# Two more logits products on GpSimd in place of VectorE, and a new stored order for about 110 other operations

## The chip, the core and the metric

The kernel runs on one core of one Trainium2 chip. The time is that of the core on the device in microseconds (us). A core has five engines that run side by side, each through its own list of instructions in order: TensorE (PE in the profile, with its weight loads as PEld), VectorE (DVE), ScalarE (ACT), GpSimd (POOL) and SyncE (SP). SP, ACT and POOL also issue DMAs, and such a DMA has a place in that engine's list.

## What is computed

For 2048 rows x of 640 numbers, the output is a gated mix of an attention and of a filter in the frequency domain:

```python
g = sigmoid((x * gate_w).sum(-1, keepdims=True))
# a: 32 heads of 20; each row attends to itself and to 7 earlier rows, 2 apart
q, k, v = split(x @ wqkv)
logits[s, w] = q[s] . k[s - 2 * w] * 20 ** -0.5     # w = 0..7, -1e9 where s - 2 * w < 0
a = (softmax(logits) @ v) @ wo
# b: a filter on the 2-D spectrum
b = irfft2(rfft2(x) * (w_r + 1j * w_i), s=(2048, 640))
out = g * a + (1 - g) * b
```

## The kernel before, in words

**Tiles.** Row 16 p + j of x lies on partition p in group j, so there are 16 row groups j of 128 partitions, even ones (par 0) and odd ones (par 1) apart, because attention goes 2 rows back at a time. The 640 columns of q, k and v come in four parts of 160.

**Stages.** First the input is folded and loaded, and from there to about 230 us PE multiplies x by wqkv (tiles qkv, in pairs of a high and a low part for accuracy); ACT copies the results out (ev) and sends them to DRAM (qkvd). `attend(par, h)` then reads k, q and v of half a part back and does the attention of it on DVE, POOL and ACT. Its names carry a number u = 4 * par + h // 2 and a letter, a for even h and b for odd: kt5a, q5a, L5a, pr5a and pv5a belong to (par, h) = (1, 2), those with 5b to (1, 3). From about 230 to 347 us `freq(g)` (line 637) filters frequency group g for g = 1, 2, 3, 0, 4 to 15. Then PE multiplies the filtered rows back (`spatial`) and the attention's output by wo (`project_even`, `project_odd`), and the mix is stored to 453.8 us.

**Logits.** In `attend` the eight rows of a partition go in four steps jj = 0, 2, 4, 6. Each is one product pr of 128x1280 numbers (k by q, line 532 and on), then a reduction on DVE into L. A step listed in the table POOL_PR has its product on POOL, which reads q from SBUF. The others are on DVE: ACT first copies the piece of q into one of three parts of a PSUM bank (qbank), and DVE multiplies from there:

```python
            if jj in POOL_PR.get((par, h), ()):
                mul, qj = G.tensor_mul, q[:, jj : jj + 2]
            else:
                self.qturn = (self.qturn + 1) % 3
                mul, qj = V.tensor_mul, self.qthird[self.qturn]
                A.copy(qj, q[:, jj : jj + 2].rearrange("p j c -> p (j c)"))
                qj = qj.rearrange("p (j c) -> p j c", j=2)
            mul(pr, w, qj.unsqueeze(2).broadcast_to([128, 2, 8, HC]))
```

After the four steps come the largest logit m (DVE), L - m on POOL, the exponential on ACT, the sum s on DVE, L * s on POOL, and then the products with v: for each jj two halves of one tile pv on POOL, which DVE reduces to a piece of o. The pieces go by DMA on SP to DRAM (od), and `project_even` and `project_odd` read them back as ot, transpose them on PE (oTp) and split them into oT (ACT copies the high part, DVE takes the rest).

**A frequency group.** `freq(g)` copies columns of zg into zc (ACT), multiplies by bt into v and u (PE), copies v to vs (ACT), adds and subtracts them into ab (DVE) and multiplies by the table mm into x and z (PE). ACT writes x into P and both, with signs, into X, and sends X to P by two DMAs on ACT's queue that exchange the two halves of the partitions. POOL then multiplies P by the filter (`P<-P,wp`, 963 columns, with the exchanged part) and adds two of its thirds (`P<-P`). DVE takes z * wp minus a third of P, and makes the two halves of s by adding and subtracting P and z. PE turns s back by the g matmuls, and ACT copies these into zg. Group 0 takes no exchange and has extra matmuls ix and iz. Where a listing numbers the tiles, P of groups 1, 2, 3, 0, 4 and so on are P_607, P_618, P_631, P_645, P_661, and of groups 8 to 12 P_714, P_727, P_741, P_754, P_767. z, x, X, vs and s of a group have numbers next to its P: X_621 is group 2's, vs_639 group 0's, zc_651 group 4's.

**The order.** Nothing is issued as the code runs. Each engine call is recorded by a Plan (line 164 and on), then the recorded calls are put into an order that is stored as packed text in ORDER, a list of which of the calls left comes next, and issued in that order by one line (385), which is why every row of the profile carries L385. The five engines' lists are this one order split by engine. Tiles come from rings of few buffers, so an operation also waits until the buffer's former tile has been read: 2 for pr and for pv, 6 for k and v together, 3 for L, 2 for q, 2 for zc, 1 for vs.

Of the kernel before, what the change touches and what calls it, by code (L numbers as in the profile page):

```python
# [201 lines left out]


ORDER = """
T>t<81poj4|NsC0{{R31`zHT%QmDPnN2o4pqG()raQ#vzl-5Q;_f%qBd^O|&eY9QYNBMzhpDJzgbo`p?)i=NlGkg4pi)v=r_Ivh`ry`@DAn{UL<7u-|?Aw}>x~K3VSb)B{-t!WAHm))%
unAhPz4I@-2Iqv#r6L>*Xc$=jvaqQRa3b^|A+Y|WKIEEj)A@6T&9m8<23aOsCR{jD@6j{sYkO?P$b#=n<341!34nZ(X=zG8UQ{qx&71|KC<t@Gco9Z^27=SGu?TP9^_xx9CA@>m7>f!s
OYWHey&#0g11et`Jku?peeD*XENp#NW~XmY)%EME)U$cKF-Z+vV9cFqn%}p&i5#r2B6?^!L$|KiDwS5{;Iff+MQp5qs5Z*^S1D?*FMGw`(SU6f9U%OiawS(-I{rACR8a0gV^g7l@8l@~
HzRC&nZHU65UcUOIO2OqBvnhaDtej1FV1NTEP#T^)e}_RXD9Ad$LgUK7O`DNW0Ah#+vteaZ7c}l&kv=txQ?dKiO=nUU)rA`8g}=!rq`Zp$UL}3=^*VzL;nRihjg*C<t}3f%b%>5e(rGT
7-9+d=Oy~il~(PiH+y=E9&IDY*4qH(EzJ@9f5sB<6JsOb8wgocoqVcb9ZqwjK27E(DzK)a!$n^bod6w(!li>{GgdFyCb^9iu%ubjZcf$uR^!DIu<=bFg$M~+%M&!@`CRf64gryh?xA;L
=GNZz41miwBNJRJ$_PkjO#GJm*8$7Wigq;fww-$@)=FqJsud(o66Kud*z2J1AyupW9GFt;JT~7#Xc;~qw*2h&<S<LPTrE0Tvv;yIwrz$dgfpLZm!26FS+ez!;5Pt$ymK)}uVU7^YB(23  # L210
abfI)oPtr{Wh!}VC7Toq2amz>-c68x1BbhR&{(ROO)>dDpl%@SkBwsg>XhKMqNltvxU8}VnLD-Mepq&s&h0shElS}Kp$)vXuTq>iX>Cb3wH*5XM0KNCE>o-pp4<I`M~`Jd4t7#L9b*fF
wuGdJat(T)z>igeMB8%*RWQ2i06@>6iiY1>U5b|2v0EKBb^l^DfU!qWovI!Z)z_$mF)>18`>*Fx>5l*lLUh^2W>YVO>m}WBw^64&l77+nuC39&CM|*NV;F&Kj^Ppbsxdr{UH3QiDdtoE
>9^Z^(}BqP7lK<BR!aE$l*Cn@sqW=Rrb62!JRq@AUQ**c44zhaQ@t%%#OaD#xOULbqH7cNBRcpC$<;6ezVESAzEV6VDilz>dquhr&==?Ggiw{Z9m#%FDOMWi=7=f>RgP8@SK-o)kAgWc
@(~x_1gJz+dYwk6|3WH!Q+8xdEtnm+stHe=6)34-WpZL}4ugdfpv6H=3ArGy{O4l+-$ydmOvz{guh;2O#|DKW?>s2?n#?x#3TACjF=U2+g*kOcry4r$vD>c_(rzX7C1gGLLs}3NQZAtv
ogzd_!bABa9T?T3Gs=$zHA+BgpwKT1x1UyIm=uw*eDoI2ukgn(P$?v&8zZ+rqRW+=JglNr!n`th?ETZV$#&=i{iwkUtIaB@Q}*NHX-6O2z+m$sMuH>Wz2^1n{cpGSFz=vH&jcSfoL*PT
l(e3=1WK!@5fXav8#wz>T7U{iN<IAmx<(?^C_>kP7N|hYIekD3RBcpw0FDjy^s|gj!DtD#|Fe=A_=*%<#m8R@<Wb!hJG2mfgFIL-rE+7}MD)%GRQf34Eqq=3$hY_fP({XdfJ|XhJkGh*
;rddl98_KAxC_7a!PrDj$BdC~u?on-Sr!%7x<Xb-%|fGLYD;nbsQhFH`ZV2!AwjD5oZh`s>-nQReDf92g(!@sE)9XSby_X}JZC};N5m{&=tv2y?|{U!Xo}XY=9BhrsO)i~RVAUM^Zq|O
U<q^R{Fq9K0g(^bS~-#Ar7l~w9U*|gOjae1XA9=)^;WNww^WC#4NH>zmLFJ{KLbF2L~M-}VOHY45$&O!e^N2K+6x=vhq?zH#-*SPa7QY%j-TtZnWJ-SP%t-ngyr>5zN0GFY5WDlJ6xVY
J{?Q+DnkgL|4!{Sm<~W1m{#H-i#v+$kXc^Td=7heyIz#Z=u004G<&&-oRvQN>@ufMHq^=_nd~Lslju>7E|fryCi!(_@>ZcR_(2!-ffb6vQBf?!jJJpypg#Pl(ICI9d_*^JoFXsY5wOvi
nr1gFTCsh?1Z_h$3nMfvh8Bme$@%=-h{q?O6}Gk2hmQOegP}ygA~^2Iy=xmWVhfbR01Yc(!EMjd<%9@Vb+3e~4Tp1v+AlQ*{#c5SAYU<n*kAABp<2#cQRW!xhkP$v4+Q_B@o1RR^qZ=!  # L220
KeYQb+1wyz!xaZ;$|p~0Rkw(@l$#UaI{9@wGRt=OVop%vdH&C)f#pnq8#sp}eaD-%4T)cljwr&kWt(1u-yr$^T9|Th^!}&q#YLBhX4!=WaHOIid?(#4<cxl{;tI|VZp<8Df0tkOj5Jg<
zrLM3bspM%T&FVXAT;ePvu{w0-b6_nx;Ueyvynjx&1|1+Tr@Ma=vsZ;Z%(dMHq!G`SSXA%hUbZ0h8CW*EQ16manzQK<G&iL$@&h?N+WhK;95=}$gl<@C*;vSR+Gf_uMhDwcnrx&(<w#E
4@wDP2Sfe^s<4LS9>wv^@!P~EXoURBZ3aW7O{<DH;@bA%XV!^Nl&1lOHC+tpbjZ+jlWz(<xS8p*U7aet(m%YtU&)nda#i2(JfPWkJVFa(3Ltu6dk!#zpbcN{))aMKqsS^Al8l>OF@O~e
x(u+`_%sPsRi0Dl>z$t3^_s&-5k^L24nD#imbvd3lI5somyD;SGYh5p&x~Eea*h2|SPh0<Eb)zkO*`v;lUxAdI~a{fLZN`^G~L~t=1sbS`R;PB!Rn>VoOf64#iStA<yF-d%C;StyT|aY
?D(Tvdj)-E5H7x(%n1xC9d_foxjYSU#`BetY+t-WLnF^a<<=FUKyU@t&wUZ+iyz%aL&8WAup}SL^6`w!wyvn?Wk95WtV9^<2QqBYqe*mJR6-|}h$TGSv<76T!0?!B3R*cOCQAQQsOxdd
m3p$Nr6FlsqZm6&X5wW3>VG@o8cE)9LE34q+962yQajx~L(yyIq<`x{dWPvVOR`<6m}Oj6rZ{<H#`=rZh;|nIj|%8ORTVkOwbj3lhBGbTy@{(rh)-RVDCFQCvIW<2(5~_J)mPX>q56=+
Lhb>Ury!q;u}317-G@VQbSrO2)@wK#*2ey?$}g#2?U)pHv2s)pO?NC$NEZW}_=Pt^aCWSUnecEhx+Ibb?goExm{@-C0R=icvA>d;Lu2H0!_EaXeEKyk9iDqL+QBxor42ZIwFnnqAn6U3
_*)I?j(1Tb0Wru}z21ORZ9XANGt|a9GXRlDTv}|*ARx}4_pIOCIo}-%!+7EO46gQUoEI60HjiILM*_ON0>z=h9(a6jQ;n(if?QQ-d^(IxQa#o>X6Jj%Q~CVQ#tLzt$>!Z+m~oDjH=b%d
EKH_NEnnRB9(XVoDJ*@Zl675mh^pl-iALQ<c#u_7Xo3rfzTZrwxLLtlJ3eToG_xzP!s~I?WSCvyaR;y760%i;da_`9s~x8jv}!Cc#!nD;$8oY;%>}(Xu+}@7MrUZ2xihJzmNgd4?UuqQ
lj=2;{2MzSWldas;&S-TwvkI_^2-P(=+cY8NZ&KM#is{cx5Azh%rCCt_psh>;~#?CtG3B{ge&v5h$2|y{1|MIAK}+Ozghda1$mEgjpr7gMG`_IAOyi2domcj>9vTFM{B)wg*vp8$43or  # L230
Z@f{5Aex(=<zM8D2QRnY(Y^KUX#@f4ZMpYmdi0Miez?%sJ5zGB^D45Fhf?kY{c@1$1BZ*>*+bO7a5u<wOeml`7Zq-=5UqRs_6{m%aRem&IUXR;KBV&N!gweQb9B4c1dkV?z||S$8Y3m`
GISu@RzcTi>)y3qbD1XFKrjX8vHIl7reyxUS`UQ^$iw2TW_U_EB}KkdFu=o|xj{SS9^$%*xDiw}`^K^#mLU;ock7`j`Qj(AEx_NJ_6u4orvtlP9ztAo9qI(|9tWj!A}E0dnKUdKnFwf7
zGmMtKJ1JmDDk~OP7f@*?4vAi$S~Y7QPj-j!`A{ShO;R91xRW^h3#^2+-prcKnN-wL2y2hR88R2htAU;VrO5f#&*@5Bx#>?5C4ph2%gxeNLs<$8e4ZgeQr~$iv#P~$&<JH_MQ%5B)~mR
{qzhlVEVEvM0r60xftwa->^J+OYgZKQ8Ieli{hlUl(tt=31MC3VNY@y-W>Mj&!KTpf7+g&#28y108c2U0qHc4VnD^$I;|}w$0CN*1p_Gc8rT2bkG2*
"""


# [729 lines left out]
```

## Time and profile before

| | us |
|---|---|
| time, median of 3 runs | 454.48 (454.02 to 456.01) |
| time of the profiled execution | 455.9 |
| its span | 453.8 |
| PE busy | 440.5 (97%) |
| PE's weight loads | 390.1 (86%) |
| DVE busy | 410.4 (90%) |
| POOL busy | 364.4 (80%) |
| ACT busy | 212.4 (47%) |

The profile shows one execution; its clock was 1.000 throughout. A row of a timeline gives the start in us, the duration, the engine, the line, the operation, the tile written and the tiles read, the sizes, and how many instructions the row holds. A bracket at its end is idle time of that engine just ahead of it, with what ended it. Tile names stand without their numbers, so it is the time that tells which group's P a row is. For example, the first product `P<-P,wp` is group 1's, the second, at 249.93 us, is group 2's, and group 8's to 11's begin at 296.56, 302.13, 307.05 and 314.62 us.

### The profile page before, as it was taken

The page shows a single profiled execution, that of the slowest core. Times are in us where ns is not written, and L with a number is a line of the kernel's source. Part 1 is how long each engine was busy: PE and PEld are TensorE (multiplying, and loading weights), DVE is VectorE, ACT ScalarE, POOL GpSimd, SP SyncE. Part 2 cuts the span into 40 slices and gives each one's busy share as a digit, 9 for nine tenths or more (in the row PEclk, how much of TensorE's full clock was granted, in tenths as well). Part 3 has the DMA queues.
Part 4 walks back from the last instruction along what each step waited for, and adds up shares of the span by engine and source line. Part 5 has one row for each costly group of instructions (what it writes and reads, how often), then busy time and mean ns, then how long its engine had stood idle before and what let it go on. Part 6 is the DMA issues. An engine that isn't in the chain of part 4 may idle for free. (4 is left out here: it accounts for less than half of the span.)

```text
span 453.8 us, 7246 instructions
## 1 busy us (share of the span) xinstructions
PE 440.5 (97%) x2440; PEld 390.1 (86%) x2440; DVE 410.4 (90%) x519; ACT 212.4 (47%) x561; POOL 364.4 (80%) x316
## 2 busy tenths in 40 slices
...
GB/s 317 389 370 285 380 300 379 244 252 284 230 192 259 364 243 315 171 243 315 311 207 290 258 269 262 287 222 315 264 241 105 82 97 59 127 193 137 282 133 87
...
## 3 DMA queue, kind: packets, MB, share of 16 engines
...
q8 instruction: 19, 0.31, 0.3%
...
## 5 line engine op out<-in xcount | busy, mean ns | idle before, releaser
L385 PE MATMUL qkv<-w,xo 128*128 128x480 f32 (+1 forms) x480 | 110.9, 386 | 0.3 <-ACT zg L385 0.3
L385 PE MATMUL qkv<-w,xe 128*128 128x480 f32 (+1 forms) x474 | 104.3, 381 | 0.0
L385 PEld LDWEIGHTS qkv<-w,xo 128*128 128x128 f32 x480 | 89.8, 189 | 14.3 <-ACT zg L385 0.7
L385 PEld LDWEIGHTS qkv<-w,xe 128*128 128x128 f32 x474 | 89.2, 188 | 14.8 <-ACT xe L385 0.6
L385 ACT COPY ev<-qkv 128x480 f32<-128x480 f32 x64 | 34.8, 556 | 39.7 <-PE qkv L385 31.8
L385 PE MATMUL woa<-wo,oT 128*128 128x320 f32 x240 | 47.2, 318 | 0.5 <-ACT oT L385 0.3
L385 PE MATMUL wob<-wo,oT 128*128 128x320 f32 x240 | 46.9, 315 | 0.2 <-ACT ya L385 0.2
L385 POOL TENSOR_TENSOR P<-P,wp 128x963 f32<-128x963 f32 (+1 forms) x16 | 35.3, 2209 | 6.8 <-DMA P<-X 4.7
L385 PEld LDWEIGHTS woa<-wo,oT 128*128 128x128 f32 x240 | 37.7, 188 | 1.4 <-ACT oT L385 0.6
L385 PEld LDWEIGHTS wob<-wo,oT 128*128 128x128 f32 x240 | 37.8, 188 | 0.6 <-ACT ya L385 0.4
L385 POOL TENSOR_TENSOR fx<-fx 128x160 f32<-128x160 f32 (+1 forms) x16 | 12.8, 817 | 24.0 <-DMA fc<-in_t_fc 16.9
L385 POOL TENSOR_TENSOR w<-raw,w 128x480 fp32r<-128x480 f32 (+1 forms) x20 | 24.8, 1263 | 5.1 <-ACT w L385 5.0
L385 ACT CAST oT<-oTp 128x384 fp32r<-128x384 f32 (+1 forms) x32 | 13.4, 428 | 31.4 <-PE oTp L385 14.6
L385 PEld LDWEIGHTS g<-mm,s 128*128 128x128 f32 x150 | 21.1, 190 | 8.0 <-ACT zg L385 5.6
L385 PE MATMUL g<-mm,s 128*128 128x128 f32 x150 | 23.9, 281 | 3.6 <-ACT zg L385 3.4
L385 DVE TENSOR_TENSOR oT<-oTp,oT 128x384 fp32r<-128x384 f32 (+1 forms) x32 | 15.3, 487 | 10.5 <-ACT oT L385 10.4
L385 PE MATMUL oa<-gt,zg 128*128 128x161 f32 (+1 forms) x96 | 24.0, 344 | 0.0
L385 PE MATMUL ob<-gt,zg 128*128 128x161 f32 (+1 forms) x96 | 22.1, 344 | 0.0
L385 PE MATMUL v<-bt,zc 128*128 128x240 f32 (+2 forms) x96 | 21.1, 325 | 0.4 <-ACT vs L385 0.3
L385 ACT CAST w<-raw 128x480 fp32r<-128x480 f32 (+1 forms) x30 | 17.3, 594 | 8.1 <-PE qkv L385 3.6
L385 PE MATMUL u<-bt,zc 128*128 128x240 f32 (+2 forms) x96 | 20.1, 322 | 0.7 <-DVE ab L385 0.7
L385 DVE TENSOR_TENSOR fx<-fx 128x642 f32<-128x642 f32 (+2 forms) x24 | 19.2, 800 | 0.7
...
## 6 DMA issues: line engine op xcount, KB each, us to landing
...
```

What stands on the lines that cost most here:

```text
L385: p.dve.memset(w, 0.0)
```

## The change

Two products go from DVE to POOL: step 6 of (1, 2), which is pr5a_539, and step 2 of (1, 3), which is pr5b_553. Each loses its ACT copy into qbank with that, and the turn of the three parts of qbank shifts for the products behind them. ORDER is replaced. The diff, with the rows of ORDER left out:

```diff
 ORDER = """
-T>t<81poj4|NsC0{{R31`zHT%QmDPnN2o4pqG()raQ#vzl-5Q;_f%qBd^O|&eY9QYNBMzhpDJzgbo`p?)i=NlGkg4pi)v=r_Ivh`ry`@DAn{UL<7u-|?Aw}>x~K3VSb)B{-t!WAHm))%
...
+T>t<81poj4|NsC0{{R31`zHT%QmDPnN2o4pqG()raQ#vzl-5hnLq{ymHQ_m(N;DL&CnVBYQJLIDZaDVocntPmM`}KpdWmwn_3?8E%N_JbolqfM<5D_C5$*_I@mj}(nvb!eyu8$`^ATPb
...
 """
...
-POOL_PR = {u: (6,) for u in ((0, 3), (0, 4), (0, 5), (0, 7), (1, 0), (1, 1), (1, 3), (1, 4), (1, 5), (1, 7))}
+POOL_PR = {u: (6,) for u in ((0, 3), (0, 4), (0, 5), (0, 7), (1, 0), (1, 1), (1, 2), (1, 3), (1, 4), (1, 5), (1, 7))} | {(1, 3): (2, 6)}
```

What the new order does is read from a listing of each engine's instructions, before against after. A minus marks a place of before, a plus one of after.

The first place is ACT's list near the exchange of group 2, about 243 to 246 us: P_618<-X_621 are its two DMAs, zc_651 the copies for group 4, vs_639 group 0's copy, wo the split of the projection's weights.

```order
 L385 COPY vs_625<-v_624 128x321
-L385 DMA P_618<-X_621 64x642 x2
+L385 DMA P_618<-X_621 64x642
 L385 ACTIVATE zc_651<-zg 128x48x4
 L385 COPY zc_651<-zg 128x48x4
+L385 COPY vs_639<-v_638 128x321
 L385 ACTIVATE g<-z 128x16
 L385 COPY zc_651<-zg 128x384
 L385 CAST wo_332<-wor_338 128x320
+L385 DMA P_618<-X_621 64x642
```

Of the two DMAs one stays and one goes behind six operations, among which the vs copy of group 0 is itself new at this place.

The second is POOL's list at the same group, about 250 to 258 us: the product and the add of group 2 and the products pv7b of attention (1, 7).

```order
 L385 TENSOR_TENSOR P_618<-P_618,wp_611 128x963
+L385 TENSOR_TENSOR pv7b_495<-vt7b,L7b 128x8x80
 L385 TENSOR_TENSOR P_618<-P_618 128x321
 L385 TENSOR_TENSOR wo_334<-wor_339,wo_333 128x320
+L385 TENSOR_TENSOR pv7b_495<-vt7b,L7b 128x8x80
 L385 TENSOR_TENSOR L6a<-L6a,m6a 128x256
-L385 TENSOR_TENSOR pv7b_495<-vt7b,L7b 128x8x80 x2
```

One half of pv7b goes between group 2's product and its add, the other behind the next split of weights.

The third is POOL's list where the two products come in, about 295 to 315 us: P_714 is group 8, P_727 group 9, P_741 group 10; L6b and pv6a belong to the attention before.

```order
 L385 TENSOR_TENSOR P_714<-P_714 128x321
+L385 TENSOR_TENSOR pr5a_539<-kt5a,q5a 128x1280
+L385 TENSOR_TENSOR L6b<-L6b,s6b 128x256
+L385 TENSOR_TENSOR P_727<-P_727,wp_718 128x963
 L385 TENSOR_TENSOR pv6a_514<-vt6a,L6a 128x8x80
-L385 TENSOR_TENSOR P_727<-P_727,wp_718 128x963
 L385 TENSOR_TENSOR P_727<-P_727 128x321
+L385 TENSOR_TENSOR pr5b_553<-kt5b,q5b 128x1280
 L385 TENSOR_TENSOR pv6a_514<-vt6a,L6a 128x8x80
 L385 TENSOR_TENSOR P_741<-P_741,wp_732 128x963
 L385 TENSOR_TENSOR P_741<-P_741 128x321
```

L6b's multiply by s6b, which stood ahead of group 8's product, is now behind its add; group 9's product goes ahead of half a pv6a; and the second moved product stands ahead of group 10.

DVE's list loses the two products, and its neighbours keep nearly the same sequence. On SP, the write of the last piece of o4a to od moves from ahead of the load of ot_1012 to between the loads yi_978 and ot_1028, about 418 to 427 us. On PE the v and u matmuls of the first groups trade places with matmuls of qkv_7, about 235 to 240 us, and single matmuls trade neighbours later; on ACT a zg copy of group 1 goes ahead of group 3's exchange. The rest are trades of neighbours in the first 20 us and in the attention up to 230 us.

More of the change, by code (lines that the diff above doesn't have):

```diff
@@ L209 @@
[L209 to L212, printed above, removed]
@@ new lines @@
+qiv+2${(+J`J5BC03mBvd0J#h>e{o09Igi!7MY@^&jdHmMw<gIh_Hqp)g=%#%_<5qZFmiqLe7xKC4h>sV(H?O7rsCo>uD)&71iZIG&0~PMs1xe2{#uY&3TNo3;yrHdzAWj;Y2#>aw8R*
+g8F9gbv_wI<SUjP$XZcCZKd{>ynpqx1)xsBO0cyE&ul`dc<RMhehUK~3VG+z_|8+Xj>lK3@PR0XYRnicmc?+67cpigIa(HsdmtkDeA0(Nch(m~81Cp^36Ew8<y;q*LD(5U!21_FWA`K+
+sbiJBtqeNk)L?%q%of@Nxi-q;U8Ml^V0f2g&t+Ntn-kI97LT}fpTg-yq=9DQ#RgsV0aH)DobPPz7*)v^!4`=|r<fe0MrAaql(&*sPm&TyOSFZsxd5i#KTTF%J%K|Q#zXdV+UkHC=CRL+
+Tp-YOQPdgDnrC3DY^^B!Mb%rH-9lM`4}s|lnVXY+GAF0`umZNZVa6KN6UW%n;nNK6KlnTMRnY(i`Gqk9D^rVAL-KS@6!HjGHWeUca8N5sf<{?%glI%EkgtIQlwp!9GpIt)ncDc{Mf4up
@@ new lines @@
+OR>VCT`xml#P_ldmlNNatj-vkWnwy?JFyjVd@NyWDBrW{_PLG4yXBsY8f5U2D;Z*=uc4Z|x@P;|#@AC{#vd%;Yg+2V+;q{)D@F8hh(_CNdj&WfqaTTSdIkzA{C=8i|E`+m>3yiLWx^!<
+sC^bC^G1dolH00Z&;-qrk_*`)LB6Ym6ba>tsTOT@sQgh8b!jQbG%#q*Q-yc_D)4HSqjCktD{9)^untTujHO+Xnsl%JcviLE3=IzNsd42D<A4qgrr+$s5Uz|GZj(t7bLLt_6M&4BY9Dtp
+t=={%J)jstVwQ6Q<7ZOvy`8741oZVi3NbegwrDw`l(<{}iy$)bw$X;JPZxssUS13b&o89gYOC>>27#)Uf$Ejg_ON>!IIx$DqkLJ;HJKb*L=zm+uZyfaSYN-!^*%cn(RFr=9(@#0Eqec8
+Qt{x0nEf6YLaUuQM!26WtB@VNap{}bh@KRqmW`EyVAku%%R@nK+w)9oj@KqYFpR2^U_YL%zO)yTTr~nkaer(=Xy7t%Xymflog3kIR$BOLrhnUE)AI(Nni}XYkQ>cmm7rIiIbTzWX6z#v
+)Lp0)sf3y4K#3fG*vPmsCkaH^vpEtV^*(F7sZ>nK*v9PcSoxsW+Fz_~BlL8X5WKK!=9DP;oZc&=4(%C;xb163)%0B|If%K0RG+s2iI-csa_<!ZBV)TD?Rv6Z;vFORbcUl?Db_~9E~kiB
@@ new lines @@
+LRy+%wsfD1xYfzdF0O2DMAjRAdiisw&v+g<Ta{4G2nR|IMd`uqR~@N2(=<wd0wH!VO4IBtj8@_2ago4!;S9^74jO$34Pg6n`*_A)tpxAa9hJMqeY8$qsW+83Hsk|-0$$hU(AO*|xAAID
+3<$-c-;GS{VyKCb!{a0u2;_WYi98BReWixxw`u8tDmR)zfmh-fdC$<StG%=Rm^NOvVl8nA&-W<m$;N)%@3kaA&sk7}Yt+>04250<!*n2pkhgtQ`=G}1;fFUFhtW^V#tAtzCHCJeYPpgb
+F`vq(=@zV_A2$K&k=O2;!FHBz6Ta%gZX_7p%TNAqC!#NSq&1-^$yY^PlF;HpWL;({BN)~Bw8T>JMILF>cl#8xykPqHMZ^}+(0}lm2gs8g`z=@&`D1aYh^vtAy;Z^PQQM80iMX9R571Z;
+LynK5nwG(u4`s~dzds&u{X&$pra}sV<ip@feCha=7KlYn`e|!|Xy^7}y^q1|e<GC>{l+Xw(P%~W9bUkrewczs$C3BAX$@aJGmPSm8OLZ70LlNzPO<5-wG58$I}=?7mCe#aMNk}M5QLrs
@@ new lines @@
+Vvv#DL+&pc^vvlmt(#|tc!yV$BP<g8-$af<<BWQJooR@BIQChI&bIoKT|s=&i=`eFM7#F$>Ug{9zfKee3F$K>a;pCxh3>e~r|YK#d$|6GA)gGbLC{sKen_!M2eA*HHuhmksB%)m5drhR
+6wHLCKWUgs(NPJ#1+B+<JBI?Hy${svjd(XsvA=$EYYv8%@4w%q#G1X?*Xw^z(k*#n-V5jYBkU}HLvoS}jZ-?d+ltFS;(`<Ya7U_;u0Ajh1GHlrl62H`FySSnsK@6Daxeezz+nWpwyqgK
+%&B`-ixK~jK_^JCsEaRiF^GQElZDpS#U)QyrDnmb+4&5umlj3NY;60WDU=cbJEhs9AxU$LOJ)AIH)cDKU+!2e=onVOVN(M**F{k(MWukxFO*^PX;s*v*trjFzl(f{Zb~D^Kvgy!)rc_k
+C%84^-IPuKygA}<4r-aME~y<Y3K|N*4wgk^g=SmsdWEx<qb_o>Vs~zB8se_;+Ah$LE|E;*u#t(r3c#|{5thDodhfxL@kBukHW=hOkbDWZNi8iisjm~ciG--(DO7i^WWTc@=I{;O%YFB%
```

39 lines of the change are left out of this document (13 added, 26 removed).

## The prediction

> **What bounds the kernel now.** I read the head of the page first, then the busy time of the engines in stretches of the run, because an average over stages with different limits decides nothing. Then I read the timelines of the engines around the places where the order changes.
>
> The first two lines are from the page.
>
> ```profile
> span 453.8 us, 7246 instructions
> ...
> PE 440.5 (97%) x2440; PEld 390.1 (86%) x2440; DVE 410.4 (90%) x519; ACT 212.4 (47%) x561; POOL 364.4 (80%) x316
> ```
>
> The next rows are the windows view: start and end of a stretch, its length, the busy time of PE, PEld, DVE, ACT and POOL in it, the granted clock, the DMA share and GB/s.
>
> ```profile
> 20.00:230.00 210.00, 209.68 (x1038) 183.08 (x1038) 202.21 (x191) 90.94 (x238) 183.93 (x160) 1.00 0.86 284
> 230.00:265.00 35.00, 31.46 (x165) 25.86 (x164) 32.49 (x46) 22.98 (x69) 30.62 (x28) 1.00 0.89 265
> 265.00:295.00 30.00, 29.90 (x195) 27.61 (x194) 28.70 (x48) 20.54 (x57) 27.21 (x21) 1.00 0.90 276
> 295.00:325.00 30.00, 28.81 (x185) 25.78 (x184) 26.53 (x43) 19.24 (x53) 22.87 (x17) 1.00 0.81 255
> 325.00:347.00 22.00, 19.45 (x127) 16.85 (x126) 21.45 (x33) 10.90 (x30) 21.09 (x16) 1.00 0.79 243
> 347.00:409.00 62.00, 62.00 (x390) 56.67 (x389) 55.52 (x75) 30.11 (x79) 54.14 (x44) 1.00 0.35 103
> 409.00:453.80 44.80, 40.65 (x282) 39.54 (x281) 31.00 (x68) 6.45 (x16) 21.98 (x25) 1.00 0.50 162
> ```
>
> PE has work back to back from 20 to 230 us (0.32 idle) and from 347 to 409 (none). Nothing that DVE or POOL does there can shorten the run as long as PE stays fed. PE waits only in the frequency stage: 35.00 - 31.46 = 3.54 us in 230 to 265, 0.10 in 265 to 295, 1.19 in 295 to 325 and 2.55 in 325 to 347, together 7.38 us. That sum is the most that a better order in the middle can win without taking work off PE. The products that leave DVE stand in the third of these places, where PE idles 1.19 us and POOL 30.00 - 22.87 = 7.13.
>
> **The change, first part: the second exchange of group 2.** This is the front of the frequency stage, where PE waits most. The rows are POOL's, then DVE's, PE's and ACT's (ACTq is ACT's DMA queue), from their timelines.
>
> ```profile
> 249.93 2.23 POOL L385 TENSOR_TENSOR P<-P,wp 128x963 f32<-128x963 f32 x1
> 252.24 0.75 POOL L385 TENSOR_TENSOR P<-P 128x321 f32<-128x321 f32 x1
> ...
> 254.37 2.65 POOL L385 TENSOR_TENSOR pv7b<-vt7b,L7b 128x640 f32<-128x640 f32 x2
> ...
> 257.75 2.23 POOL L385 TENSOR_TENSOR P<-P,wp 128x963 f32<-128x963 f32 x1
> ```
>
> ```profile
> 253.46 0.89 DVE L385 TENSOR_TENSOR s<-P,z 128x321 f32<-128x321 f32 x2
> ...
> 260.02 0.50 DVE L385 TENSOR_TENSOR z<-z,P 128x321 f32<-128x321 f32 x1 [0.69 <-POOL P L385]
> ```
>
> ```profile
> 244.10 1.11 PE L385 MATMUL v<-bt,zc 128*128 128x240 f32 x6
> ...
> 254.10 0.68 PE L385 MATMUL g<-mm,s 128*128 128x128 f32 x4
> ...
> 260.97 0.81 PE L385 MATMUL z<-ab,mm 128*128 128x321 f32 x2 [0.52 <-DVE t L385]
> ```
>
> ```profile
> 243.39 0.43 ACT L385 COPY vs<-v 128x321 f32<-128x321 f32 x1
> 243.47 1.12 ACTq L385 DMA_DIRECT2D P<-X  x2
> ```
>
> The pair at 243.47 is group 2's. In the new order its second half stands behind three zc copies, the vs copy of group 0, the g activation and a cast. The vs row shows how a DMA stands to the operation ahead of it: it was issued 0.08 us after that copy began, so it need not wait for the copy's end, only for whatever holds up the copy's start. The last of these in the new order is the vs copy of group 0, which needs the v matmuls of 244.10, done at 244.10 + 1.11 = 245.21. So the half goes out at about 245.4 instead of 244.0. When it lands is read from the tile view of P for the three pairs around it (groups 1, 2 and 3): the issue rows, and under each the time to landing.
>
> ```profile
> L385 ACTq DMA_DIRECT2D P<-X x2: 468/498/529, 236.5 to 237.2; - x2
> DMA to landing us min/median/max: 5.9/6.6/7.3
> L385 ACTq DMA_DIRECT2D P<-X x2: 469/539/609, 243.5 to 244.0; - x2
> DMA to landing us min/median/max: 4.3/4.3/4.3
> L385 ACTq DMA_DIRECT2D P<-X x2: 507/545/583, 250.2 to 250.8; - x2
> DMA to landing us min/median/max: 4.5/5.4/6.4
> ```
>
> With its own 4.3 it lands at 249.7, ahead of POOL's product at 249.93: nothing is lost. With the middle of the six, (4.5 + 5.9) / 2 = 5.2, it lands at 250.6 and POOL starts 0.7 late; with the longest, 7.3, at 252.7 and 2.8 late. No gain can come of it, since POOL got to the product at 249.93 without waiting.
>
> Beside that, half of pv7b's two products (2.65 / 2 = 1.33) is put between this product and its add. The add then ends at 252.24 + 0.75 + 1.33 = 254.3 even without a late landing, DVE's first s of group 2 (0.89 / 2 = 0.45) at 254.8, and PE's g matmuls, which stood at 254.10 with no idle time ahead of them, start 0.7 late. PE ran without a wait from there to the z matmuls of group 4, and these had 0.52 to wait anyway; they go from 260.97 to 261.15. So the half product alone costs 0.2. A late landing of d us moves both, the g matmuls and POOL's next product (257.75), on which DVE's z - P (260.02, a wait on POOL of 0.69) and so the z matmuls depend: the price is d + 0.2. The vs copy that goes earlier, and a zg copy that goes ahead of group 3's exchange, let PE's v and g start sooner, but PE then waits at the g matmuls for s, so I give them nothing. Ends: +0.2 at the pair's own landing and +3.0 at 7.3. The pair's own is the nearest row, the six together say +0.9; I take +0.5. What DVE and POOL do next (the reduce of pv7b, group 3's product) follows the same delay, so nothing later in this stretch hides it.
>
> **Second part: the two moved products.** The rows are POOL's and then DVE's, in 295 to 335.
>
> ```profile
> 295.98 0.63 POOL L385 TENSOR_TENSOR L6b<-L6b,s6b 128x256 f32<-128x256 f32 x1 [1.91 <-DVE s6b L385]
> ...
> 300.85 1.42 POOL L385 TENSOR_TENSOR pv6a<-vt6a,L6a 128x640 f32<-128x640 f32 x1 [1.22 <-DVE o6a L385]
> ...
> 307.05 2.24 POOL L385 TENSOR_TENSOR P<-P,wp 128x963 f32<-128x963 f32 x1 [0.46 <-ACT X L385]
> ...
> 310.75 1.38 POOL L385 TENSOR_TENSOR pv6a<-vt6a,L6a 128x640 f32<-128x640 f32 x1 [0.63 <-DVE o6a L385]
> ...
> 314.62 2.27 POOL L385 TENSOR_TENSOR P<-P,wp 128x963 f32<-128x963 f32 x1 [2.50 <-DMA P<-X]
> ...
> 331.97 2.93 POOL L385 TENSOR_TENSOR pr5b<-kt5b,q5b 128x1280 f32<-128x1280 f32 x1
> ```
>
> ```profile
> 303.49 1.48 DVE L385 TENSOR_TENSOR pr5a<-kt5a,qbank 128x1280 f32<-128x1280 f32 x1
> ...
> 313.06 0.49 DVE L385 TENSOR_TENSOR z<-z,P 128x321 f32<-128x321 f32 x1
> ...
> 318.74 0.49 DVE L385 TENSOR_TENSOR z<-z,P 128x321 f32<-128x321 f32 x1
> ...
> 320.53 0.56 DVE L385 TENSOR_TENSOR oT<-oTp,oT 128x384 fp32r<-128x384 f32 x1 [0.31 <-ACT oT L385]
> ```
>
> A product costs 2.93 us on POOL (331.97) and 1.48 on DVE (303.49): POOL gets 5.86 more, DVE 2.96 less, and ACT loses two small copies that nobody waits for. POOL's waits in the rows above come to 1.91 + 1.22 + 0.46 + 0.63 + 2.50 = 6.72, so the work fits, if its order lets it. It mostly does. L6b's second multiply, with its 1.91 of waiting for DVE, now stands behind group 8's product, add and the first moved product, so POOL can begin group 8 as soon as its exchange is there. Group 10's product (307.05) is the one that is pushed. Ahead of it come the second moved product and half a pv6a, and by adding up POOL's own durations from group 8 on it begins near 310.0 and ends at 312.3. DVE reads it at 313.06: 0.8 us are left. Group 11's product starts at about 312.3 + 0.75 (its predecessor's add) + two half products of 1.3 = 315.7 and ends at 318.0, 0.7 ahead of DVE's read at 318.74.
>
> On DVE the freed 2.96 us only count where DVE itself is what PE waits for. Its next wait after the second product is for ACT (the oT copy, 320.53), which waits for PE's transposes, so an earlier DVE meets that wait earlier and stands in it longer. PE's whole idle time in this stretch is 1.19 us. What is left is s of group 11, which can come up to 0.6 sooner. Ends: -2.96 if all of it reached the end, and +1.0 if POOL runs over the 0.8 and 0.7 that I count for it by about as much again. I take -0.3, near the 0.6 rather than the 2.96, because the stretch's PE row allows no more than 1.19.
>
> **Third part: the last piece of od in the tail.** Rows from SP's queue, the tile view of od from 380 on (reads and writes together) and PE.
>
> ```profile
> 425.35 0.32 SPq L385 DMA_DIRECT2D yi<-ad  x1
> 427.27 0.32 SPq L385 DMA_DIRECT2D ot<-od  x1
> ```
>
> ```profile
> DMA to landing us min/median/max: 1.7/3.2/5.7
> ```
>
> ```profile
> 435.16 0.49 PE L385 MATMUL oTp<-ident,ot 128*128 128x128 f32 x3
> ```
>
> The write of o4a's last piece moves from an early place in SP's queue to directly behind the load of 425.35, so it goes out at about 425.7, and the read of 427.27, which needs what it writes, can go when it has landed. At the median that is 425.7 + 3.2 = 428.9, and the read is in at 428.9 + 3.2 = 432.1, 3.0 us before PE's transposes at 435.16. At the longest twice it is 437.1: +1.9. I take 0, with the ends 0 and +1.9; SP's later loads and stores stand 1.6 us later for a while, under PE's projections.
>
> **The rest** (qkv matmuls traded with v and u on PE about 230 to 242, folds and loads in the first 20 us, single places elsewhere) lies where PE had 209.68 of 210.00, or swaps neighbours of under 0.6 us: 0, with 0.3 to either side.
>
> Sum: 0.5 - 0.3 + 0 + 0 = +0.2. The profiled execution took 455.9 us, of which 453.8 are span and 2.1 lie around it; by it the changed kernel takes 456.1. It lies 1.4 above the median of the three runs, 454.48, so against the median the forecast is 454.7.
>
> **The rivals.** About 0.5% (2.3 us, so 452.2 to 456.8) is what a measurement of this kernel can tell from no change.
>
> Faster, because DVE sets the pace of the second half. For it: DVE has 90% of the span on the page and 21.45 of 22.00 in 325 to 347, where PE idles 2.55 for it. DVE's 2.96 us would then come off whole, 454.48 - 2.96 = 451.5; it decides if the freed time is still there at 325. Against it: the waits for ACT lie in between. I give it 0.27, with 0.20 for a gain over 2.3 us. The Trainium skill, in Perfetto Trace Analysis, section Identifying the Most-Contended Engine, says to rank Vector, Scalar and GPSIMD by their occupancy and Tensor by its LDWEIGHTS busy share rather than its matmul busy share, and to optimise the highest first. By that rule DVE's 90% leads PEld's 86%, and this rival is what it foretells; PE's 62.00 of 62.00 in 347 to 409 speaks against reading it over the whole run.
>
> Slower, because group 2's second exchange lands late. Its place is POOL's product at 249.93 and its price d + 0.2: with the 7.3 of the pair before it, +3.0 - 0.3, so 457.2. It decides from a landing at 245.4 + 6.9 = 252.3 on, where 252.3 - 249.9 + 0.2 - 0.3 comes to the 2.3; below that the delay stays within the half per cent. Three of the six neighbours took 5.9 or more, one over 6.9. Chance 0.18, with 0.10 above 456.8.
>
> Slower in the tail: both transfers of the third part take 5.7, +1.9 beside the +0.2, so 456.6. It decides once the two take 9.5 together. Chance 0.08, with 0.02 above 456.8.
>
> **How the numbers follow.** The forecast, no change that can be told, has the remaining 0.47, with a range of its own of 453.4 to 456.2. Faster by over 0.5%: 0.20. Slower: 0.10 + 0.02 = 0.12. Within: 0.68, being 0.47 + 0.07 of the first rival, 0.08 of the second and 0.06 of the third. The range reaches into the first rival to 451.8, short of its whole price, and into the second to 457.0; about 0.1 is left out on each side.
>
> **What would show it.** Right: the exchange of group 2 issued near 245.4, POOL's product within a microsecond of 249.93, half a pv7b before its add, and PE's g matmuls some 0.7 later than 254.10; DVE with longer waits for ACT and PE in 305 to 325 and two products of 2.93 more on POOL, ending before DVE reads groups 10 and 11; PE back to back from 347 on, and its transposes at the tail not waiting. Wrong: POOL waiting over 2 us on the exchange; PE's idle in 295 to 347 falling by over 2 us (then DVE was the bound); or PE waiting on POOL's P where I count 0.8 to spare.

## The result, and the profile after

The changed kernel took 458.49 us in the median of 8 runs (456.52 to 461.67), the kernel before 455.31 in 8 runs beside it (454.02 to 457.25). The ratio is 1.0072, with a 95% interval of 1.0051 to 1.0092: slower by 3.2 us, where no change was forecast (454.7, range 451.8 to 457.0). Of the 3.8 between forecast and measurement, 0.8 is that the kernel before itself came to 455.31 here and not to the 454.48 that the forecast started from. The ratios here and below leave out four executions that took over 1.5% more than the fastest of their kernel: one of 1133 us, and three of 460.3 to 462.6 us at a mean clock of 0.993 (kt4b's load later, group 3's wp later, products back on DVE), which the last column of the table below does count. The profiled execution took 457.86 us with a span of 456.0, 2.0 and 2.2 more than before. So the profile shows about two thirds of the loss, and the rest has to be looked for in the other executions.

The engines' shares from the page of the changed kernel, then its windows by stage (columns as above):

```profile
span 456.0 us, 7248 instructions
...
PE 439.2 (96%) x2440; PEld 390.0 (86%) x2440; DVE 407.4 (89%) x517; ACT 211.0 (46%) x559; POOL 369.3 (81%) x318
```

```profile
20.00:230.00 210.00, 209.49 (x1039) 183.06 (x1038) 202.46 (x192) 90.78 (x239) 183.91 (x160) 1.00 0.87 285
230.00:265.00 35.00, 29.87 (x160) 25.01 (x158) 30.82 (x43) 21.22 (x65) 29.17 (x28) 1.00 0.82 248
265.00:295.00 30.00, 29.20 (x189) 26.76 (x188) 28.52 (x48) 19.83 (x56) 28.85 (x22) 1.00 0.90 267
295.00:325.00 30.00, 28.43 (x183) 25.72 (x182) 23.99 (x41) 19.29 (x52) 26.15 (x19) 1.00 0.84 254
325.00:347.00 22.00, 19.89 (x129) 17.27 (x127) 20.91 (x31) 11.32 (x31) 20.11 (x14) 1.00 0.83 253
```

PE's idle time in 230 to 265 grew from 3.54 to 5.13 us, and in 295 to 325 from 1.19 to 1.57. DVE got its relief there (26.53 to 23.99) and POOL its work (22.87 to 26.15), but nothing came of it. PE's rows with a wait, from its timeline, tell where:

```profile
241.56 0.78 PE L385 MATMUL z<-ab,mm 128*128 128x321 f32 x2 [1.01 <-ACT X L385]
...
256.59 0.68 PE L385 MATMUL g<-mm,s 128*128 128x128 f32 x4 [3.00 <-DVE s L385]
...
265.96 0.64 PE L385 MATMUL u<-bt,zc 128*128 128x240 f32 x2 [0.70 <-DVE ab L385]
...
297.78 0.94 PE L385 MATMUL g<-mm,s 128*128 128x128 f32 x6 [0.19 <-ACT zg L385]
...
317.70 0.81 PE L385 MATMUL z<-ab,mm 128*128 128x321 f32 x2 [1.35 <-DVE s L385]
...
326.67 0.94 PE L385 MATMUL g<-mm,s 128*128 128x128 f32 x6 [0.20 <-ACT zg L385]
```

Set each against its row of before. The z matmuls at 241.56 stood at 241.99, with the same wait of 1.01, so PE was 0.43 early there. The u matmuls with the wait of 0.70 stood at 264.29, so they are 1.67 late. The g matmuls that waited 0.59 at 296.51 are 1.27 late: 0.40 of that wait was swallowed. Those at 324.51 are 2.16 late, and the span ends 2.2 late. There are two steps: about 2 us at the g matmuls of group 2, and about 1.4 at the z matmuls of group 12, with some of it given back between.

The first step on POOL, and the two DMAs that belong to it, from the timelines of POOL, ACT's queue and SP's:

```profile
251.71 2.23 POOL L385 TENSOR_TENSOR P<-P,wp 128x963 f32<-128x963 f32 x1 [3.75 <-DMA P<-X]
253.89 1.35 POOL L385 TENSOR_TENSOR pv7b<-vt7b,L7b 128x640 f32<-128x640 f32 x1
255.16 0.75 POOL L385 TENSOR_TENSOR P<-P 128x321 f32<-128x321 f32 x1
```

```profile
245.05 0.47 ACTq L385 DMA_DIRECT2D P<-X  x1
```

```profile
244.93 0.33 SPq L385 DMA_DIRECT2D wp<-in_ws  x1
```

```profile
DMA to landing us min/median/max: 6.6/6.6/6.6
```

The half that was moved left at 245.05 (245.4 was forecast) and took 6.6 us to land, not 4.3. POOL, with nothing else to do, waited 3.75 for it. The load of wp for group 3, 642 KB, went out 0.12 us ahead of it. In the kernel before, the same load went out at 246.93, 2.95 behind it:

```profile
246.93 0.33 SPq L385 DMA_DIRECT2D wp<-in_ws  x1
```

The load has no new place in SP's list. In both profiles it goes out 0.03 us after POOL's product of group 1 ends, and that product waited long for its own exchange in the one and hardly in the other (before, then changed):

```profile
244.66 2.24 POOL L385 TENSOR_TENSOR P<-P,wp 128x963 f32<-128x963 f32 x1 [2.24 <-DMA P<-X]
```

```profile
242.66 2.24 POOL L385 TENSOR_TENSOR P<-P,wp 128x963 f32<-128x963 f32 x1 [0.19 <-DMA P<-X]
```

So POOL was 2.00 us earlier at group 1, and without the late half it would have begun group 2 at 251.71 - 3.75 = 247.96, ahead of before. The wait took that back, and 1.78 more. In the twelve profiles of the experiments below, the product of group 1 begins between 241.69 and 244.86: the profile of before is one of the late ones.

The second step, on POOL, on SP's queue, and the time to landing of group 10's exchange (issued at 304.8 and 305.3):

```profile
297.95 2.95 POOL L385 TENSOR_TENSOR pr5a<-kt5a,q5a 128x1280 f32<-128x1280 f32 x1
...
309.76 1.38 POOL L385 TENSOR_TENSOR pv6a<-vt6a,L6a 128x640 f32<-128x640 f32 x1
313.63 2.26 POOL L385 TENSOR_TENSOR P<-P,wp 128x963 f32<-128x963 f32 x1 [2.49 <-DMA P<-X]
```

```profile
300.92 0.73 SPq L385 DMA_DIRECT2D kt4b<-qkvd  x1
```

```profile
DMA to landing us min/median/max: 6.8/7.3/7.8
```

POOL was ready for group 10 at 311.14 (the sum had 310.0, and PE stood about 1.3 late by then), and then waited for the exchange, which had needed 2.5 to 2.7 us in the kernel before. The load of kt4b, 600 KB, had started at 300.92. Before, it stood at 304.99, just when DVE's pr5a product of 303.49 ended, because kt4b takes the buffer of kt5a, which that product is the last to read. On POOL the product ended at 300.90. So the moved product let a load go 4.07 us earlier, ahead of an exchange.

### The profile page after: what moved, and what is told of

Its sections match the earlier page's. It is cut to its first block, busy times and chain, and to the rows that moved or that the text cites. A ratio compares the mean times of both kernels' runs of the same rounds, so it can differ in the third digit from the quotient of the medians.

```text
span 456.0 us, 7248 instructions
## 1 busy us (share of the span) xinstructions
PE 439.2 (96%) x2440; PEld 390.0 (86%) x2440; DVE 407.4 (89%) x517; ACT 211.0 (46%) x559; POOL 369.3 (81%) x318
```

## The experiments

Twelve kernels ran, one of them the changed kernel again, each 10 to 12 times beside 33 to 35 executions of the kernel before on the same chip. There were three chips, and the kernels of one chip share its executions of before. The table gives the ratio with its interval, then, from the profile of one execution, how long the second half of group 2's exchange took to land and how long POOL waited for it, and PE's longest wait between 230 and 350 us. The last column counts the executions with a mean granted clock under 0.998, and is explained further down.

| kernel | ratio (95%) | half landed in, POOL waited | PE's longest wait | clock under 0.998 |
|---|---|---|---|---|
| before | 1 | 4.3, 0 | 1.01 | 9 of 103 |
| changed | 1.0072 (1.0051 to 1.0092) | 6.6, 3.75 | 3.00 | 6 of 8 |
| changed, again | 1.0042 (1.0011 to 1.0074) | 6.2, 4.09 | 2.57 | 6 of 12 |
| group 2's pair restored | 1.0008 (0.9976 to 1.0039) | 5.1, 1.10 | 1.01 | 4 of 12 |
| pairs of 2 and 14 restored | 1.0002 (0.9974 to 1.0029) | 4.3, 0.04 | 1.89 | 5 of 12 |
| kt4b's load later | 1.0022 (0.9992 to 1.0051) | 3.3, 0 | 0.94 | 6 of 12 |
| pair restored and kt4b later | 1.0024 (1.0001 to 1.0046) | 4.7, 0 | 1.39 | 7 of 12 |
| group 3's wp later | 1.0045 (1.0022 to 1.0069) | 2.9, 0.21 | 2.39 | 6 of 12 |
| all four | 1.0037 (1.0012 to 1.0063) | 3.1, 0 | 1.91 | 7 of 12 |
| products back on DVE | 1.0011 (0.9981 to 1.0040) | 5.3, 3.23 | 1.70 | 3 of 11 |
| before, half one step back | 1.0005 (0.9981 to 1.0029) | 4.6, 0.35 | 1.23 | 2 of 12 |
| before, half two steps back | 1.0058 (1.0031 to 1.0085) | 6.0, 4.21 | 2.48 | 6 of 10 |
| before with the two products | 1.0012 (0.9995 to 1.0029) | 4.5, 0 | 1.06 | 0 of 12 |
| the same, kt4b later | 1.0011 (0.9988 to 1.0034) | 3.9, 0 | 1.04 | 1 of 12 |

**Group 2's exchange as a pair again.** On ACT's list of the changed kernel:

```diff
 DMA P_618<-X_621
+DMA P_618<-X_621
 ACTIVATE zc_651<-zg
...
 CAST wo_332<-wor_338
-DMA P_618<-X_621
```

> The changed kernel with one DMA put back: the second half of group 2's exchange goes directly behind its first half on ACT's queue. Theory (two exchanges that land late, group 2's and group 10's, make the loss): POOL's product of group 2, which waited 3.75 us in the changed kernel's profile, waits under 0.5, PE's wait of 3.00 at the g matmuls of group 2 falls under 1.2, and the time falls by 1.2 to 2.2 us, to a ratio of about 1.003 to the kernel before. Rival (the 5.86 us more work on POOL is the loss, wherever the transfers land): the front gets shorter but the end stays within 0.5 us of the changed kernel, ratio 1.006 to 1.008.

The ratio is 1.0008 and the median 455.08, 3.4 below the first measurement of the changed kernel. POOL waited 1.10 at 248.09, PE not at all at the g matmuls. One DMA, put back by six places, takes away nearly all that the first measurement had shown of the loss; against the second measurement, below, the intervals overlap. The bound given for POOL (under 0.5) was missed, and the time fell by more than the 1.2 to 2.2 us expected.

**The same kernel again, and both pairs.** The first is the changed kernel unchanged. The second restores the pair of group 14 too, whose second half had also been moved back on ACT's list.

> The changed kernel itself once more, for a second profile and to stand beside the others on one chip. Theory (the moved half of group 2's exchange lands at times before and at times after POOL wants it, and longer waits of PE are at times followed by a stretch of half clock): ratio 1.005 to 1.009; in the profile either POOL waits over 1 us at group 2's product and PE over 1 us at its g matmuls, or the profiled execution is as fast as the kernel before. Rival (a steady cost of the moved products): the profile loses the 1 to 2 us in 295 to 325 whatever group 2 does.

> The changed kernel with two exchanges put back as pairs, group 2's and group 14's (its second half too had been moved some 4 us back on ACT's list); the moved products and kt4b's early load stay. Theory: most of the loss is in these transfers, so the ratio is 0.997 to 1.002 and executions under full clock are as rare as for the kernel before. Rival (the moved products, with the early load, cost 1 us or more): ratio over 1.003.

The changed kernel came out at 1.0042, a little under its own expectation, and its second profile has the same event at the same place: the load of wp at 244.47, the half at 245.44, 6.2 us to landing, POOL waiting 4.09 and PE 2.57. This time there was no wait for group 10's exchange worth naming (0.64, and put down to ACT) and none at group 12. With both pairs the ratio is 1.0002; group 14's pair adds nothing that can be told from group 2's alone. What was expected of the clock did not come: 5 of 12 executions ran under 0.998, against 4 of the 35 of before beside them.

**The load of kt4b held back,** alone and with the pair. On SP's list:

```diff
-DMA kt4b_574<-qkvd
 DMA wp_745<-in_ws
 DMA ad<-ya_834
+DMA kt4b_574<-qkvd
```

> The changed kernel with one load moved: kt4b goes behind the next two entries of SP's list, so that its 600 KB start some 7 us later, behind group 10's exchange instead of 4 us ahead of it. Theory: the exchange of group 10 lands in 2.5 to 5 us instead of 7.8, POOL's wait of 2.49 at group 10's product goes to under 0.5, PE's wait of 1.35 at the z matmuls of group 12 goes, and the time falls by 0.8 to 1.6 us, to a ratio of about 1.004. Rival (POOL's added work): POOL reaches groups 10 and 11 no sooner than DVE reads them, so the wait stays over 1 us and the time within 0.4 us of the changed kernel, ratio 1.006 to 1.008.

> The changed kernel with both moves at once: group 2's exchange as a pair again, and kt4b's load behind group 10's exchange. Theory: the two losses lie apart and add, so the time falls by 2 to 3.6 us, to a ratio between 0.998 and 1.002. Rival (POOL's added work, or the hundred other moves): ratio still over 1.004.

Neither came out as the theory had it. Group 10's exchange still took 6.3 and 6.5 us with the load held back, and 2.6 and 5.5 in the kernel with the pair; with the load alone held, POOL still waited 1.30 at group 10's product, though that is put down to ACT. What the edit did was to let the next load of wp, 642 KB, into kt4b's place. It went out at 301.17, ahead of both halves of the exchange (301.20 and 301.72), and in the kernel with the pair at 303.42, between them (303.22 and 303.76), where the half ahead of it took the 2.6 and the half behind it the 5.5. PE's wait at group 12 was gone in both, but it was gone in the second profile of the changed kernel as well. With the pair restored, holding the load gives no gain: 1.0024 against 1.0008, with intervals that overlap. The second step of the profile is thus real in that one execution, but it is not shown to cost time on average. The interval of the load alone, up to 1.0051, overlaps with that of the second measurement and reaches the lower bound of the first, and its profile happens to be one in which group 2's half was issued 0.87 us ahead of wp's load (244.20 against 245.07) and landed in 3.3.

**The two products alone, in the order of before,** and then with the load held back. On POOL's list:

```diff
 TENSOR_TENSOR P_714<-P_714
+TENSOR_TENSOR pr5a_539<-kt5a,q5a
 TENSOR_TENSOR pv6a_514<-vt6a,L6a
...
 TENSOR_TENSOR P_727<-P_727
+TENSOR_TENSOR pr5b_553<-kt5b,q5b
```

> The kernel before with the two products alone on POOL, behind the add of group 8 and behind the reduction of the first of them, and q4a's load moved back to where its buffer is free; the rest of the order as before. Theory: DVE's 2.96 us turn into waits, kt4b's load starts some 4 us earlier and meets group 10's exchange, which lands 2 to 4 us later; POOL's product of group 10 and DVE's z - P behind it come about 2 us later and the time rises by 0.5 to 1.5 us, ratio 1.001 to 1.003. Rival (the products are the loss): ratio 1.005 or more. Other rival (DVE sets the pace): ratio 0.994 to 0.997.

> As the run with the two products alone on POOL, and kt4b's load moved two entries back on SP's list, behind group 10's exchange. Theory: group 10's exchange lands in 2.5 to 5 us again, what is left is POOL's 5.86 us more in its idle time, ratio 0.998 to 1.001. Rival (the load has no part in it): the same ratio as the run without the load's move, within 0.001.

Both came to 1.001, 0.5 us, with an interval that just holds no change; the load has no part in the time, as the rival said. It has one in the exchange, as the theory said: behind the load of kt4b (301.32 against 302.42) the two halves of group 10's took 5.0 and 5.1 us, and with that load at 305.39 they took 2.5 and 2.6. But POOL never waited for them here, because its own list kept it busy. What there is of a loss shows in PE's rows, here of the products alone:

```profile
307.56 0.81 PE L384 MATMUL z<-ab,mm 128*128 128x321 f32 x2 [1.06 <-DVE s L384]
```

It comes from DVE's z - P of group 9 behind the first product on POOL (POOL's product of group 9 stood at 302.52 to 304.79):

```profile
304.83 0.50 DVE L384 TENSOR_TENSOR z<-z,P 128x321 f32<-128x321 f32 x1 [2.51 <-POOL P L384]
```

So the freed DVE time did turn into a wait, and the added POOL time can do harm where a group's product stands behind it. Neither the gain of 2.96 nor a large loss is there.

**The products back on DVE, in the changed order,** with their two copies:

> The changed order with the two products back on DVE, with their two copies on ACT, at the places they had before; everything else as in the changed kernel. Theory (the loss is in the other moves of the order): the same time as the changed kernel within 0.8 us, ratio 1.003 to 1.008, and as many executions under full clock. Rival (the products are the loss): ratio 0.999 to 1.002.

The ratio is 1.0011 with an interval up to 1.0040. That is under the 1.003 that was expected and within the rival's bounds, though in its profile the half again lands late (5.3 us, POOL 3.23, PE 1.70). The interval overlaps with that of the changed kernel's second measurement, so it does not say how much of the loss is the products'. Against that measurement it allows anything from none to all of it. With that of the first, from 1.0051 on, it does not overlap: by the ratio alone, putting back the two products takes away as much as putting back the one DMA.

**The kernel before with only the half moved,** one step as in the changed order, or two steps, behind the copies for group 5. On ACT's list, the second:

```diff
 DMA P_618<-X_621
-DMA P_618<-X_621
...
 COPY zc_666<-zg
+DMA P_618<-X_621
 CAST wo_333<-wor_339
```

> The kernel before with one DMA moved: the second half of group 2's exchange goes behind the copies for group 4, the g activation and the cast, as in the changed kernel; nothing else. Theory: it is issued about 1.0 to 1.4 us later, lands over 5.5 us after its issue, POOL waits 1 to 2 us for it at group 2's product, and the time rises by 0.6 to 1.8 us, ratio 1.001 to 1.004. Rival (the long landing in the changed kernel's profile was chance): it lands after about 4.3, POOL does not wait, ratio 0.999 to 1.001.

> The kernel before with the second half of group 2's exchange moved still further back on ACT's list, behind the copies for group 5, so that it goes out about 3 to 4 us later than before. Theory (PE's wait at group 2 is the price, and longer waits of PE are at times followed by half clock): the half lands at 251.5 or later, POOL waits over 1.5 us, PE over 0.8 at the g matmuls, the time rises by 1 to 2.5 us and more than 4 of 12 executions run under a mean clock of 0.998. Rival (the delay is taken up by POOL's and DVE's other work, and the clock depends on other moves): ratio under 1.002 and at most 2 of 12 executions under 0.998.

One step back costs nothing that can be told from the noise: the half left at 245.87, took 4.6 us, and POOL, which was not ready for it before 250.20, waited 0.35. The theory's bounds for the landing and for POOL were missed, and the rival nearly held. Two steps back cost as much as the whole change, 1.0058. These are the rows of that kernel, POOL's first:

```profile
252.72 2.22 POOL L384 TENSOR_TENSOR P<-P,wp 128x963 f32<-128x963 f32 x1 [4.21 <-DMA P<-X]
```

```profile
256.44 0.68 PE L384 MATMUL g<-mm,s 128*128 128x128 f32 x4 [2.48 <-DVE s L384]
```

With no product moved and no other operation out of place, a group 2 that becomes ready at 252.7 instead of 249.9 gives PE a wait of the same size at the same matmuls, a loss of the same size, and as large a share of executions under a lower clock (6 of 10). The theory held here, with the 1.0058, 2.6 us, a little over its 2.5. So a late group 2 is enough for the loss. But this is a longer step than the change's own: the half went out at 246.63, against 245.05 and 245.44 in the changed kernel. The change's own step, taken alone in the order of before, showed no cost, so it needs something else of the new order to do its harm.

**Group 3's wp behind the half,** and all four edits at once:

```diff
-DMA wp_622<-in_ws
 DMA ot_816<-od
+DMA wp_622<-in_ws
 DMA mm_649<-in_t_mm
```

> The changed kernel with one load moved: wp of group 3 (642 KB) goes one entry back on SP's list, behind the read of ot0, so that the moved half of group 2's exchange is issued ahead of it. In the two profiles of the changed order in which that half took 6.2 and 6.6 us, this load was issued 0.1 to 1.0 us ahead of it; in the profile in which it took 3.3, 0.9 us behind it. Theory (a bulk load issued just ahead of an exchange is what makes it late): the half lands within 4.8 us of its issue, POOL waits under 1.5 us for group 2 and PE under 1.2 at its g matmuls, the time falls by 1 to 2 us, ratio 1.000 to 1.004. Rival (the half is late because it is issued late, whatever goes ahead): it still lands after 6 us or more and the ratio stays at 1.004 to 1.008.

> The changed kernel with four places put back or moved at once: the exchanges of groups 2 and 14 as pairs, and the loads of wp of group 3 and of kt4b behind the exchanges they met. Theory: with all four the moved products cost nothing and DVE's relief is free to count, ratio 0.995 to 1.000. Rival (the order's other moves or the products cost something steady): ratio 1.002 or more.

For the half itself the theory held: ahead of the load it landed in 2.9 us, and POOL waited 0.21. But the ratio stayed where the second measurement had it (1.0045). The read of ot at 247.22, the load at 247.64 and mm's load at 248.85 now went out ahead of group 3's exchange (249.27 and 250.79), and that one took 6.9 and 7.3 us:

```profile
DMA to landing us min/median/max: 6.9/7.1/7.3
```

```profile
258.20 2.22 POOL L383 TENSOR_TENSOR P<-P,wp 128x963 f32<-128x963 f32 x1 [2.99 <-DMA P<-X]
```

```profile
261.40 0.81 PE L383 MATMUL z<-ab,mm 128*128 128x321 f32 x2 [2.39 <-DVE t L383]
```

The same happened with all four edits (1.0037, as the rival had it): group 3's exchange took 7.8 and 6.8, POOL waited 2.51 and PE 1.91. In these two profiles the delay had been handed to the next exchange. That it is what keeps their ratios up is not shown: the profile with the 2.39 took 455.12 us, no more than the 455.29 of before beside it, and the interval of the four edits overlaps with that of the pair alone.

**The clock.** Executions under 0.998 were slower than the others of the same kernel, in the medians by 0.8 to 4.5 us, mostly by 2 to 4. Four profiles caught the stretch in question. First the kernel with both pairs restored, in windows of 2 us (start and end, length, busy time of the five engines, granted clock, DMA share, GB/s):

```profile
258.00:260.00 2.00, 0.39 (x2) 0.34 (x3) 0.68 (x2) 0.24 (x1) 0.69 (x1) 1.00 0.97 311
260.00:262.00 2.00, 2.00 (x10) 1.88 (x9) 0.90 (x3) 1.49 (x4) 0.83 (x1) 0.58 0.61 220
262.00:264.00 2.00, 2.00 (x8) 1.60 (x7) 1.78 (x2) 0.32 (x1) 1.92 (x4) 0.57 0.06 26
264.00:266.00 2.00, 1.50 (x8) 0.98 (x6) 0.84 (x3) 0.68 (x3) 2.00 (x1) 1.00 0.30 63
```

PE was busy for 0.39 of 2 us, waiting 1.89 for mm's load, and right behind it the clock stood at 0.57 for 4 us: 2 x 0.42 + 2 x 0.43 = 1.7 us lost, on top of the wait. The kernel with the pair and kt4b later shows it twice as long, at 344 to 354, behind waits of 1.39 and 0.57:

```profile
344.00:346.00 2.00, 0.75 (x6) 0.78 (x6) 1.84 (x5) 0.47 (x2) 2.00 (x3) 0.95 0.78 238
346.00:348.00 2.00, 1.43 (x7) 1.14 (x7) 2.00 (x3) 0.48 (x1) 2.00 (x3) 0.50 0.00 0
348.00:350.00 2.00, 2.00 (x7) 1.60 (x7) 2.00 (x2) 0.37 (x1) 1.92 (x4) 0.50 0.00 0
350.00:352.00 2.00, 2.00 (x6) 1.40 (x5) 2.00 (x3) 0.43 (x1) 2.00 (x4) 0.50 0.00 0
352.00:354.00 2.00, 2.00 (x12) 1.80 (x12) 2.00 (x2) 0.70 (x2) 2.00 (x2) 0.84 0.32 82
```

That is 2 x (0.05 + 0.50 + 0.50 + 0.50 + 0.16) = 3.4 us. The kernel of before with the half one step back shows two stretches, one behind a wait of 1.01 at 241.86, the other behind waits of 1.23 and 0.57 at 346.58 and 348.05:

```profile
242.00:244.00 2.00, 2.00 (x7) 1.72 (x8) 1.97 (x4) 0.53 (x1) 1.33 (x2) 0.55 0.98 376
244.00:246.00 2.00, 2.00 (x9) 1.86 (x8) 0.30 (x2) 0.57 (x2) 1.92 (x3) 0.60 0.89 255
348.00:350.00 2.00, 1.95 (x6) 1.69 (x7) 2.00 (x3) 0.37 (x1) 1.94 (x3) 0.50 0.00 0
350.00:352.00 2.00, 2.00 (x8) 1.70 (x7) 2.00 (x3) 0.43 (x1) 1.98 (x3) 0.64 0.00 0
```

Each comes to 1.7 us, and so does one in the kernel with all four edits, at 264 to 268 behind a wait of 1.91. The wait of 1.01 is there in the profiles of before and of the changed kernel too, without such a stretch. An execution with a mean clock of 0.996 has lost 0.004 x 456 = 1.8 us in all, one such stretch; with 0.993 it has lost 3.2, two. The stretch does not follow every wait: behind the 3.00, 2.57, 2.48 and 2.39 in the table's profiles the clock stayed at 1.00.

By the same sum, which is an estimate, the executions of the changed kernel lost 2.3 us each on average to the clock in the first measurement and 1.6 in the second, the 103 of before 0.4. That is 1.9 and 1.1 us more, over half of the 3.2 and 2.2 by which the medians differ. In the second measurement the six executions at 0.998 or more have a median of 455.29 us, and the 31 such of before 455.30. With group 2's pair restored eight such have 454.54, with both pairs seven have 454.32. But with the half two steps back four such still have 457.56. These splits were made afterwards and over few executions; they suggest that at full clock the new order loses little, and gains a little where the exchange is kept together.

## Why the prediction was wrong, point by point

**What bounds the kernel** was right. PE's waits in the frequency stage are where the profile loses its time, DVE's relief gained nothing there that shows, and 20 to 230 us did not change (0.32 idle before, 0.51 after).

**First part: the step that failed is the term of +0.5, and beside it a term for the clock, which the sum does not have.** That a late landing holds up POOL, DVE and PE in turn was right, and so was its price per microsecond. The half left at 245.05 and not 245.4. By "d + 0.2", with d = 251.71 - 249.93 = 1.78, the z matmuls of group 4 should have come 2.0 late; they moved from 260.97 to 262.77, 1.8 late (the row stands below). What was mis-sized is d, which has 0.3 in the +0.5, because "the pair's own is the nearest row". That row was measured with the 642 KB of wp 2.95 us behind the pair; in both profiles of the changed kernel the load went out ahead of the half. A look at the load's row of before would not have shown it, since the half, forecast for 245.4, would still have gone out ahead of 246.93. It took the step behind that: the load starts when POOL's product of group 1 ends, and that hangs on an exchange that landed in 5.9 and 7.3 us before and in 3.2 and 5.0 in the changed kernel. With d = 1.78 the sum of the prediction comes to 1.78 + 0.2 - 0.3 = +1.7 us. The profiles differ by 2.0 and the medians by 3.2, so most of the rest is the clock's. The six neighbours' times (the longest of them gave 2.8 us of delay as the upper end) covered the landing that came: the second rival said late landing with its price, and gave it 0.18. It came about in both profiles of the changed kernel, with POOL waiting over 2 us, which the prediction had named as a sign that it is wrong.

```profile
262.77 0.71 PE L385 MATMUL z<-ab,mm 128*128 128x321 f32 x2
```

The Trainium skill, in DMA: Bandwidth & Descriptors, section Queues, rings and completion order, says that each DMA engine goes round in turn between the queues that have work for it, a packet at a time; that two queues' transfers lengthen each other is what the traces here agree with, by which one went out first: the second half of group 2's exchange landed in 2.9 to 5.1 us in the nine profiles in which it went out ahead of wp's load, and in 4.6 to 6.6 in the five in which it went out behind.

**Half of pv7b between product and add** did what was said: POOL's add began 3.45 us after the product began instead of 2.31, and DVE's s waited a further 1.09 for it. This is the 0.2 of the sum, and it was not run by itself.

**Second part.** POOL took both products in the idle time, group 8 began without L6b in front, and POOL was ready for group 10 at 311.14. "0.8 us are left" held for POOL's own list: without the wait it would have ended that product at 311.14 + 2.26 = 313.40, and DVE began to wait for it at 315.93 - 1.80 = 314.13. What the step left out is that the product is also the last reader of kt5a, so that moving it moved a load. In the first profile group 10's exchange then landed late and PE waited 1.35; the runs do not show that it costs time on average. Nor does the list of the change name two other moves: the load of q4a went from 285.72 to 311.26, and the second half of group 14's exchange from 330.04 to 335.54. The two products by themselves, with q4a's load, come to +0.5 (interval -0.2 to 1.3 us) against the -0.3 that was taken, within the +1.0 that was its upper end. The same run refutes the rival that DVE sets the pace, at its price of 2.96. Its premise was a misreading: of the 2.55 us that PE idles in 325 to 347, PE's rows of before put 0.18 down to DVE and nearly all the rest to ACT's copies.

**Third part.** PE's transposes of the tail came at 437.06, without a wait ahead of them, as forecast:

```profile
437.06 0.49 PE L385 MATMUL oTp<-ident,ot 128*128 128x128 f32 x3
```

**What no step had** is the clock. The profiles of before and of the changed kernel both show 1.00 throughout, so the loss in their medians, 3.2, is larger than that in their profiles, 2.0. By the estimate above the clock is 1.9 of the 3.2, and the sum has no term for it; the one profile that it was made from showed a clock of 1.000 throughout. The Trainium skill, in TensorE: Matmul & The Clock Gate, section What's actually happening, says that the clock is halved after at least one idle window of about 3.4 us, and that the window runs freely. The losses of 1.7 and 3.4 us here are one and two such windows at half clock, which agrees; that it comes after one wait and not after another of the same length fits a window that does not start with the wait. The page's threshold of a whole idle window does not fit: here half clock followed waits of 1.01 to 1.91 us, and PE was at work in between.

**What stays open.** With group 2's pair restored, 4 and 5 of 12 executions still ran under 0.998, against 9 of 103 before. Which of the other moves does that is not shown, nor how the loss divides between the half and the products, where the intervals overlap. Nor is it shown why the change's own step of the half costs nothing by itself in the order of before.
